# Attention and MLP on one core: exponentials of 54 score tiles written back into PSUM, with engines, buffers and order chosen anew

## The chip, the cores and the metric

The kernel runs on one core of a Trainium2 chip. The metric is the device time of one execution in microseconds (us), as the median of several runs; lower is better. The engines are named as in the profile: PE (TensorE, with PEld for its weight loads), DVE (VectorE), ACT (ScalarE), POOL (GpSimd) and SP (SyncE, which here issues every DMA).

## The reference

Four sequences of 576 tokens, eight heads of width 64, then an MLP of 512 to 2048 to 512:

```python
q_rot, k_rot = rotate(q), rotate(k)                   # rotary embedding
scores = (1 / np.sqrt(64)) * q_rot @ k_rot.T
scores = scores - scores.max(-1)
attn = np.exp(scores); attn = attn / (attn.sum(-1) + 1e-9)
x = (attn @ v)                                        # as [2304 tokens, 512]
h = x @ w_in
out = (s * np.maximum(h, 0) ** 2 + b) @ w_out         # [2304, 512]
```

## The kernel before

**Tiles.** Two heads of one sequence make a pair `pr` (16 pairs). A pair has nine score tiles `i`: eight of 128 query rows by 576 keys, and a ninth (`i` = 8) that holds the last 64 rows of both heads. That is 144 tiles. Tokens are grouped into nine MLP units of 256 tokens; a unit can start when the attention of its tokens is done.

**One score tile.** `s_tile` (L1298) multiplies on PE into one of two score buffers `s` in PSUM, each of two banks. `s_max` (L1324, DVE) scales the scores in place and gives the negative maximum `nm`. `s_exp` (L1330, ACT) takes the exponentials into a buffer `p` in SBUF and sums them into `sum`; when it ends, the score buffer is free for the next tile. `p_s` and `p_r` (L1336, L1344) make `r`, the reciprocal of the sum, in the place of `sum`. For 124 of the tiles, p times r is then split into two fp16 halves: `p_a` (L1356, on ACT, DVE or POOL by a table) writes the high half, `p_b` (L1361, always DVE) writes the remainder, both into `pab`. A DMA transpose, `p_t` (L1368), turns `pab` into `pt`, and `pv_sum` (L1384, PE) multiplies with v. The other 20 tiles, called G in the code (L773: the 16 tiles of unit 0 and the tiles 4 to 7 of pair 0), go another way in fp32: `p_norm`, `p_T` on PE, `p_ev`, `pv32`. All instructions on ACT that the helper `act` records carry its line, L1062; DVE's go by the helpers' L1054, L1056 and L1059.

**Preparation.** Every two pairs share staging buffers `st_q`, `st_k`, `st_v`. q and k are rotated (`rotate`, four instructions), scaled and split (`qk_hi`, `qk_lo`), transposed by DMA and copied with halves swapped (`swap_k`, into `kS`). The weights arrive as 64-bit values in a buffer `w64` and are turned into fp32 by `w_sign` (POOL), `w_rebias` and `w_f32` (DVE), later halved into fp16 pairs (`w_hi`, `w_lo`).

**MLP.** For each of 16 column blocks `f`, `mlp_in` (12 matmuls, L1514; unit 0 in fp32, L1511), then for each two blocks Relu and Square on ACT (`mlp_r`), `g_hi` and `g_lo` (the fp16 halves) and `mlp_out` (L1551).

**Order.** When the kernel is built, `plan` (L684) makes a list of work items, each with an engine, a cost, a due time and the tokens and buffers it reads and writes. `schedule` (L890) then goes through time with these costs and always gives a free engine the ready item with the earliest due time. The order it finds is written out as each engine's fixed instruction stream. The table `PRM` holds offsets of due times and, in `PRM['eng']`, the engine of single items; `BUFS` holds the numbers of buffers: one each for staged `k` and `q`, four for `p`, three for `g`, nine for `vS`.

Of the kernel before, what the change touches and what calls it, by code (L numbers as in the profile page):

```python
# [7 lines left out]
F32 = mybir.dt.float32  # L8
# [19 lines left out]
PRM = {'z0': -0.31,  # L28
 'z1': 0.75,
 'd': 2.86,  # L30
 'ld': -6.32,
 's_lead': 50.37,
 'pab': -0.63,
 'pvlag': -9.44,
 'W0': 5.5,
 'W1': 26.24,
 'Wd': 0.37,
 'wld': 49.09,
 'sq': -6.66,
 'WP': -4.92,  # L40
 'WPd': -2.52,
 'm0': -53.68,
 'x_lead': 54.8,
 'r_lead': 78.68,
 'outlag': 5.0,
 'bias': -24.48,
 'look': 0.034124466599701066,
 'tab': -80.57,
 'fq': (0,),
 'nF': 25,  # L50
 'vz': -4.4,
 'du': [0.25, -5.14, -4.7, -3.11, -3.9, 42.96, -2.92, 5.19, 22.68],
 'ud': 20.54,
# [12 lines left out]
         ('g_lo', 3, 12): 'DVE',  # L66
# [4 lines left out]
         ('g_lo', 8, 12): 'POOL',  # L71
         ('g_lo', 2, 0): 'POOL',
         ('g_hi', 0, 4): 'DVE',
# [5 lines left out]
         ('g_hi', 7, 0): 'DVE',  # L79
         ('g_hi', 4, 14): 'ACT',  # L80
         ('g_hi', 3, 14): 'DVE',
         ('g_hi', 5, 14): 'DVE',
# [19 lines left out]
         ('g_lo', 8, 0): 'DVE',  # L102
         ('g_lo', 7, 2): 'DVE',
# [32 lines left out]
         ('g_hi', 4, 8): 'DVE',  # L136
         ('g_hi', 1, 4): 'ACT',
         ('g_hi', 8, 10): 'ACT',
         ('x_hi', 7): 'ACT',
# [8 lines left out]
         ('g_hi', 6, 2): 'DVE',  # L148
# [3 lines left out]
         ('g_hi', 5, 12): 'ACT',  # L152
         ('g_lo', 5, 12): 'DVE',
         ('x_hi', 6): 'DVE',
         ('g_hi', 6, 8): 'DVE',
         ('g_hi', 8, 2): 'ACT',
         ('g_hi', 7, 12): 'DVE',
         ('g_hi', 8, 14): 'DVE',
         ('g_hi', 0, 8): 'ACT',
         ('g_hi', 8, 8): 'ACT',  # L160
         ('g_hi', 8, 4): 'DVE',
# [17 lines left out]
         ('g_lo', 7, 10): 'POOL',  # L179
# [3 lines left out]
         ('g_hi', 0, 2): 'ACT',  # L183
# [17 lines left out]
         ('w_rebias', 0, 4): 'POOL',  # L201
         ('g_lo', 4, 10): 'POOL',
         ('g_lo', 6, 6): 'DVE',
         ('g_lo', 8, 14): 'DVE',
         ('g_lo', 5, 14): 'DVE',
         ('g_hi', 0, 12): 'DVE',
         ('g_hi', 0, 0): 'ACT',
         ('w_rebias', 1, 1): 'ACT',
         ('w_rebias', 0, 0): 'ACT',
# [4 lines left out]
         ('g_lo', 3, 2): 'POOL',  # L214
# [5 lines left out]
         ('g_lo', 5, 4): 'POOL',  # L220
# [3 lines left out]
         ('g_hi', 2, 14): 'ACT',  # L224
         ('x_hi', 4): 'DVE',
# [19 lines left out]
         ('g_lo', 2, 4): 'POOL',  # L245
         ('w_rebias', 0, 3): 'POOL',
         ('w_rebias', 0, 13): 'ACT',
# [7 lines left out]
         ('g_lo', 7, 6): 'POOL',  # L255
# [4 lines left out]
         ('g_hi', 6, 14): 'ACT',  # L260
# [5 lines left out]
         ('w_rebias', 1, 15): 'POOL',  # L266
# [3 lines left out]
         ('p_ev', 0, 2): 'DVE',  # L270
# [11 lines left out]
         ('p_norm', 0, 2): 'ACT',  # L282
# [6 lines left out]
         ('w_rebias', 1, 10): 'ACT',  # L289
# [5 lines left out]
         ('rotate', 13, 'k'): 'DVE',  # L295
         ('rotate', 13, 'q'): 'DVE',
         ('g_hi', 5, 10): 'DVE',
# [6 lines left out]
         ('p_s', 3, 2): 'DVE',  # L304
         ('p_s', 8, 7): 'ACT',
         ('p_a', 8, 2): 'POOL',
         ('p_a', 15, 5): 'POOL',
         ('p_a', 4, 1): 'ACT',
         ('p_a', 13, 6): 'ACT',
         ('v_hi', 2): 'ACT',  # L310
         ('v_hi', 15): 'DVE',
         ('p_a', 13, 2): 'DVE',
         ('p_a', 11, 2): 'ACT',
         ('p_a', 8, 8): 'DVE',
         ('p_a', 13, 4): 'POOL',
# [5 lines left out]
         ('p_s', 10, 4): 'DVE',  # L321
# [4 lines left out]
         ('p_s', 14, 8): 'DVE',  # L326
         ('p_s', 9, 5): 'ACT',
         ('p_s', 11, 1): 'DVE',
         ('p_s', 6, 1): 'ACT',
         ('p_a', 11, 1): 'POOL',  # L330
# [55 lines left out]
         ('qk_hi', 13, 'q'): 'ACT',  # L386
# [4 lines left out]
         ('p_a', 14, 0): 'ACT',  # L391
         ('p_s', 0, 1): 'DVE',
         ('v_hi', 0): 'ACT',
         ('p_a', 7, 7): 'POOL',
         ('w_hi', 0, 7): 'ACT',
         ('p_s', 15, 3): 'ACT',
         ('p_a', 14, 3): 'DVE',
# [4 lines left out]
         ('p_s', 13, 1): 'ACT',  # L402
# [4 lines left out]
         ('p_a', 10, 1): 'ACT',  # L407
         ('p_s', 15, 6): 'DVE',
         ('p_a', 5, 8): 'DVE',
         ('p_a', 13, 5): 'POOL',  # L410
         ('p_a', 14, 6): 'POOL',
         ('p_s', 10, 7): 'ACT',
# [52 lines left out]
         ('p_s', 10, 6): 'DVE',
         ('p_s', 12, 4): 'DVE',
# [1169 lines left out]
```

## Time and profile before

| | |
|---|---|
| Median of 3 runs (lowest, highest) | 693.55 us (692.4, 694.84) |
| The profiled execution: time | 690.18 us |
| The profiled execution: span from first to last instruction | 688.4 us |
| Busy in the span: PE, DVE, ACT, POOL | 618.3, 508.0, 397.5, 166.3 us |
| Granted TensorE clock, mean | 0.954 |

The profiled execution took 1.8 us more than its span, and 3.4 us less than the median of the runs. Busy times count the time in which an engine had at least one instruction in work; matmuls overlap, so their mean duration is longer than their share of busy time. The clock is the share of full speed that was granted to TensorE. A releaser (the name behind an arrow) is what ended an idle time.

### The profile page before, as it was taken

Reading aid. Unit: us, or ns where it says so; the run is one execution under the profiler, and the core shown is the slowest. Engines: PE = TensorE matmul, PEld = TensorE weight load, DVE = VectorE, ACT = ScalarE, POOL = GpSimd, SP = SyncE. Lnnn points to the kernel's source line nnn. Section 1 sums busy time; section 2 is a strip of 40 time slices with the busy share of each in tenths; the row PEclk is TensorE's granted clock in tenths of the full one; section 3 lists DMA queues with packets and bytes.
Section 4 is the critical chain, followed back from the end, with each engine's and each line's share of the span. In section 5 each row is a group of like instructions: output and inputs, shape, how many; then the busy total and the mean of one; then the engine's idle time right before and its main releaser. Section 6 shows DMA issues by size and latency. Waiting matters only on the chain.

```text
span 688.4 us, 13122 instructions
## 1 busy us (share of the span) xinstructions
PE 618.3 (90%) x4854; PEld 399.5 (58%) x4854; DVE 508.0 (74%) x1214; ACT 397.5 (58%) x842; POOL 166.3 (24%) x162
## 2 busy tenths in 40 slices
PE   1866669999997989799999899989999999999997
PEld 1543335655565655476666466656756666676664
DVE  4389878897999997999998699889959992110301
ACT  2535447766656878578676676856646552343221
POOL 1632373311420336020114111141121030111010
PEclk9996559999999999999999899999999999999999
DMA  7475762689765589579789656988585663000100
GB/s 205 111 187 175 193 169 81 146 148 228 198 136 130 111 187 177 118 147 201 151 192 204 110 102 138 187 165 134 119 146 87 118 131 60 1 31 1 31 0 31
DMA packets 223887, 89.33 MB, mean 130 GB/s; under 512 B 193616, under 2 KB 218320, under 8 KB 223824
## 3 DMA queue, kind: packets, MB, share of 16 engines
q1 hardware_dynamic: 223824, 88.51, 60.1%
q8 instruction: 38, 0.62, 0.4%
q14 instruction: 25, 0.20, 0.1%
HBM read 31.82 MB, written 4.72 MB: 53 GB/s over the span
## 4 chain that ended last, share of the span: by engine, by line
PE 41%; DVE 9%; DMA 7%; SPq 3%; ACT 3%; issue 2%; POOL 0%; DVEq 0%; ACTq 0%
PE po L1551 17%; PE px L1514 15%; DMA pt<-pab 5%; PE px L1392 5%; PE s L1320 3%; DVE s L1327 2%; DVE pab L1059 2%; DMA st_v<-in_v_dram 1%; SPq L1192 1%; ACT hr L1062 1%; SPq L1204 1%; ACT p L1062 1%; DMA vS<-v 1%; ACT junk L1062 1%; SPq L1267 1%
## 5 line engine op out<-in xcount | busy, mean ns | idle before, releaser
L1551 PE MATMUL po<-wio,g 128*128 128x512 f16 x768 | 188.2, 381 | 0.0
L1514 PE MATMUL px<-xa,wio 128*128 128x256 f16 x1536 | 186.3, 273 | 0.0
L1514 PEld LDWEIGHTS <-wio 128*128 128x128 f16 x1536 | 148.4, 98 | 37.2 <-issue 1.7
L1062 ACT ACTIVATE p<-s,nm 128x576 f32<-128x576 f32 x144 | 105.7, 734 | 68.9 <-DVE s L1327 38.6
L1327 DVE TENSOR_SCALAR_CACHE_REDUCE s<-s,es 128x576 f32<-128x576 f32 x135 | 108.9, 814 | 6.8 <-PE s L1321 6.5
L1551 PEld LDWEIGHTS <-g 128*128 128x128 f16 x768 | 71.0, 99 | 70.4 <-issue 3.6
L1059 DVE SCALAR_TENSOR_TENSOR pab<-p,sum,pab 128x576 f16<-128x576 f32 x124 | 104.5, 851 | 9.9 <-POOL pab L1056 6.6
L1535 POOL TENSOR_TENSOR g<-hr,g 128x512 f16<-128x512 f32 x36 | 46.5, 1292 | 210.8 <-ACT g L1062 93.6
L1062 ACT ACTIVATE hr<-px,xc 128x512 f32<-128x512 f32 x64 | 43.8, 684 | 90.0 <-PE px L1514 90.0
L1392 PE MATMUL px<-pt,v 128*64 128x256 f16 (+1 forms) x860 | 53.8, 251 | 14.7 <-DMA pt<-pab 12.8
L1320 PE MATMUL s<-qkT 128*128 128x512 f16 (+1 forms) x150 | 55.2, 407 | 10.3 <-ACT p L1062 10.1
L1320 PE MATMUL s<-kS,qkT 128*128 128x512 f16 (+1 forms) x150 | 55.3, 405 | 9.4 <-DMA kS<-qkT 9.4
L1062 ACT ACTIVATE pab<-p,sum 128x576 f16<-128x576 f32 x64 | 49.0, 768 | 22.5 <-DVE sum L1346 9.4
L1059 DVE SCALAR_TENSOR_TENSOR wio<-w,wio 128x512 uint32<-128x512 uint32 x64 | 49.3, 782 | 10.5 <-POOL wio L1056 10.4
L1392 PEld LDWEIGHTS <-v 128*64 128x64 f16 x860 | 37.7, 112 | 32.2 <-issue 19.6
L1320 PEld LDWEIGHTS <-qkT 128*128 128x128 f16 (+1 forms) x300 | 29.3, 105 | 45.4 <-issue 15.2
L1056 POOL TENSOR_SCALAR pab<-p,sum 128x576 f16<-128x576 f32 x26 | 21.8, 840 | 133.8 <-DVE sum L1346 59.9
L1056 POOL TENSOR_SCALAR wio<-w 128x512 f32<-128x512 f32 x32 | 26.0, 813 | 88.3 <-DMA w<-in_moe_w_in_dram 45.4
L1062 ACT ACTIVATE hr<-hr 128x512 f32<-128x512 f32 x72 | 45.1, 626 | 1.2
L1416 DVE CAST g<-hr 128x512 f16<-128x512 f32 x29 | 13.0, 448 | 43.9 <-ACT hr L1062 43.8
L1535 DVE TENSOR_TENSOR g<-hr,g 128x512 f16<-128x512 f32 x28 | 20.7, 741 | 29.1 <-ACT g L1062 29.0
L1321 PEld LDWEIGHTS <-qkT 128*128 128x128 f16 (+1 forms) x300 | 28.3, 104 | 16.3 <-issue 12.7
(139 smaller groups left out, 926.0 us busy)
## 6 DMA issues: line engine op xcount, KB each, us to landing
w<-in_moe_w_in_dram SPq DMA_DIRECT2D x16, 512.0 KB, 4.5
w<-in_moe_w_out_dram SPq DMA_DIRECT2D x16, 512.0 KB, 4.1
kS<-qkT SPq DMA_DIRECT2D x30, 144.0 KB, 2.7
st_k<-in_k_dram SPq DMA_DIRECT2D x16, 256.0 KB, 3.1
st_q<-in_q_dram SPq DMA_DIRECT2D x16, 256.0 KB, 3.3
st_v<-in_v_dram SPq DMA_DIRECT2D x16, 256.0 KB, 4.7
out_dram<-o SPq DMA_DIRECT2D x7, 512.0 KB, 2.6
vS<-v SPq DMA_DIRECT2D x32, 64.0 KB, 2.3
```

Source lines behind the costliest of these rows:

```text
L1056: eng.tensor_scalar(out=out, in0=in0, scalar1=s1, scalar2=s2, op0=op0, op1=op1)
L1059: nc.vector.scalar_tensor_tensor(out=out, in0=in0, scalar=scalar, in1=in1, op0=op0, op1=op1)
L1062: nc.scalar.activation(out=out, in_=in_, func=func, **kw)
L1192: nc.sync.dma_start(out=t[:, 0, 0:8].rearrange("p (h t) d -> p h (t d)", h=2), in_=main.rearrange("h (p t) d -> p h (t d)", t=4))
L1320: nc.tensor.matmul(ps[rows, MAIN:2 * MAIN], lhs, kk[:, 4 * h:4 * h + 4], start=(n == 0), stop=(n == 1))
L1321: nc.tensor.matmul(ps[rows, MAIN - TAIL:MAIN], lhs, kk[:, 8, 64 * h:64 * h + 64], start=(n == 0), stop=(n == 1))
L1327: nc.vector.tensor_scalar(out=T["s"], in0=T["s"], scalar1=-1.0 / 8.0 if "qF" in st[pr] else st[pr]["es"], scalar2=None, op0=ALU.mult, op1= ...
L1392: nc.tensor.matmul(o[64 * h:64 * h + 64, 0:n], v_rows(pr, h, k, z), pv_rhs(pr, i, h, k), start=((z, k) == todo[0]), stop=((z, k) == todo[-1]))
L1416: nc.vector.tensor_copy(out, in_)
L1514: nc.tensor.matmul(ph, w16[0][:, f, wz, cc], X["xa"][:, xz, c], start=(c == 0 and n == 0), stop=(c == NC - 1 and n == 2))
L1535: (nc.vector if eng == DVE else nc.gpsimd).tensor_tensor(out=g[:, 1], in0=r, in1=g[:, 0], op=ALU.subtract)
L1551: nc.tensor.matmul(po, g[:, gz, jj], w16[1][:, f, wz], start=(f == 0 and i == 0), stop=(f == NF - 1 and i == 2))
```

## The change

1. `s_exp` takes a place `at`. Where the table says `PS`, the exponentials go back over the scores: `T["p"] = T["s"]`, in PSUM. Both `p_a` and `p_b` then read PSUM, and they list the score buffer among what they use, so that it is free only after `p_b`. For `PS`, `p_a` runs on ACT or DVE (POOL entries become ACT).
2. The table has 65 `PS` entries. Eleven of them are tiles of G, for which the code sets `SB`; so 54 of the 124 split tiles are in PSUM, 70 keep `p` in SBUF.
3. `BUFS`: `k` and `q` 1 to 2, `p` 4 to 3, `g` 3 to 2, `vS` 9 to 4; the others stay.
4. Due-time offsets in `PRM` are new, the latencies and two rates that `schedule` uses too, and many engine entries. `nF` goes from 25 to 22, which leaves the same 20 tiles in G. The number of matmuls and of DMAs does not change.

Counted over all items, the engines change so (before to after):

| step | ACT | DVE | POOL |
|---|---|---|---|
| `p_a`, p in SBUF | 64 to 50 | 34 to 7 | 26 to 13 |
| `p_a`, p in PSUM | 0 to 47 | 0 to 7 | none |
| `p_s` | 62 to 70 | 82 to 74 | none |
| `rotate` | none | 23 to 20 | 9 to 12 |
| `g_hi` | 35 to 33 | 29 to 31 | none |
| `g_lo` | none | 28 to 30 | 36 to 34 |
| `p_ev` | 11 to 13 | 9 to 7 | none |
| `p_norm` | 10 to 9 | 5 to 5 | 5 to 6 |
| `qk_hi` | 21 to 22 | 5 to 5 | 4 to 3 |
| `v_hi` | 13 to 12 | 2 to 2 | 1 to 2 |
| `w_rebias` | 19 to 18 | none | 13 to 14 |

```diff
-PRM = {'z0': -0.31, 'ld': -6.32, 's_lead': 50.37, 'pab': -0.63, 'pvlag': -9.44, 'wld': 49.09, 'm0': -53.68,
- 'x_lead': 54.8, 'r_lead': 78.68, 'bias': -24.48, 'look': 0.034124466599701066, 'nF': 25,
- 'du': [0.25, -5.14, -4.7, -3.11, -3.9, 42.96, -2.92, 5.19, 22.68], 'ud': 20.54, 'sbt': 5.22,
+PRM = {'z0': -2.03, 'ld': -2.77, 's_lead': 51.82, 'pab': -0.7, 'pvlag': -14.21, 'wld': 19.1, 'm0': 0.57,
+ 'x_lead': 68.78, 'r_lead': 117.69, 'bias': -60.48, 'look': 0.02, 'nF': 22,
+ 'du': [0.25, -5.0, -4.72, -0.78, -4.34, 55.9, 3.61, 33.52, 20.04], 'ud': 20.46, 'sbt': 2.1,
...
-         ('p_a', 8, 3): 'DVE',
+         ('p_at', 13, 5): 'PS',
+         ('p_at', 5, 0): 'SB',
...
-BUFS = {'k': 1, 'q': 1, 'v': 2, 'z': 2, 'p': 4, 'pab': 4, 'pt': 2, 'x': 2, 'xa': 2, 'r': 3, 'g': 3, 'w64': 2, 'v16': 4, 'qkT': 4, 'kS': 4, 'vS': 9}
+BUFS = {'k': 2, 'q': 2, 'v': 2, 'z': 2, 'p': 3, 'pab': 4, 'pt': 2, 'x': 2, 'xa': 2, 'r': 3, 'g': 2, 'w64': 2, 'v16': 4, 'qkT': 4, 'kS': 4, 'vS': 4}
...
-DVE_RATE, POOL_RATE = .42, .66
+DVE_RATE, POOL_RATE = .37, .62
...
-        add(n + .2, ACT, .72, "s_exp", *c, r=[("s", c), ("nm", c)], w=[("p", c)])
+        G = i < 8 and slot_of[pr, i | 3] < PRM["nF"]
+        at = "SB" if G else pick("p_at", c, "SB")
+        pk, ps = ("p" if at == "SB" else "pp", c), [] if at == "SB" else [("s", c)]
+        add(n + .2, ACT, .72 if at == "SB" else .70, "s_exp", *c, at, r=[("s", c), ("nm", c)], w=[pk])
...
-            add(z, e, None, "p_a", *c, e, r=[("p", c), ("r", c)], p=[("pab", c)])
-            add(z + .1, DVE, .73, "p_b", *c, r=[("p", c), ("r", c)], w=[("pab", c)])
+            e = ACT if ps and e == POOL else e
+            add(z, e, (.67 if e == ACT else .73) if ps else None, "p_a", *c, e, r=[pk, ("r", c)] + ps, p=[("pab", c)])
+            add(z + .1, DVE, .73 if at == "SB" else .75, "p_b", *c, r=[pk, ("r", c)] + ps, w=[("pab", c)])
+            work[-1] = {**work[-1], "port": int(at == "SB")}
...
-    def s_exp(pr, i):
+    def s_exp(pr, i, at):
         T = tiles[pr, i]
-        T["sum"] = small("sum%d" % slots["p"], 1, 1)
-        T["p"] = new(pp, "p", [P, 576], F32)
+        T["sum"] = small("sum%d" % slots["p"] if at == "SB" else "psum%d" % T["slot"], 1, 1)
+        T["p"] = new(pp, "p", [P, 576], F32) if at == "SB" else T["s"]
         act(T["p"], T["s"], AF.Exp, bias=T["nm"], scale=-1.0, accum_out=T["sum"])
```

## Rows read from the trace of the kernel before

**Rows 1.** The page: the line of the span, the busy time of each engine, and the slices of PE, DVE, ACT and the clock (40 equal slices, 17.2 us each; a digit is the busy share in tenths).

```profile
span 688.4 us, 13122 instructions
PE 618.3 (90%) x4854; PEld 399.5 (58%) x4854; DVE 508.0 (74%) x1214; ACT 397.5 (58%) x842; POOL 166.3 (24%) x162
PE   1866669999997989799999899989999999999997
DVE  4389878897999997999998699889959992110301
PEclk9996559999999999999999899999999999999999
```

**Rows 2.** Busy time by stage: the stretch, its length, busy time of PE, PEld, DVE, ACT and POOL with the number of instructions, the granted clock, the busy share of the DMA engines and GB/s.

```profile
0.00:50.00 50.00, 28.97 (x136) 18.08 (x136) 26.92 (x63) 19.91 (x40) 20.32 (x24) 1.00 0.64 169
50.00:100.00 50.00, 30.95 (x157) 16.54 (x157) 41.91 (x89) 23.36 (x51) 20.93 (x23) 0.59 0.65 179
100.00:565.00 465.00, 439.60 (x3732) 285.84 (x3733) 417.54 (x1025) 315.89 (x694) 111.92 (x105) 0.98 0.73 149
565.00:689.00 124.00, 118.83 (x834) 78.99 (x830) 21.65 (x40) 38.36 (x60) 13.14 (x11) 0.99 0.09 23
```

**Rows 3.** PE's waits between 100 and 565 us: who waited for whom, us in total, times, longest.

```profile
PE px L1392 <- DMA pt<-pab: 12.8, 12, 2.1
PE s L1320 <- ACT p L1062: 8.0, 8, 3.6
PE px L1392 <- ACT bcs L1062: 1.7, 1, 1.7
PE px L1072 <- ACT junk L1062: 0.9, 1, 0.9
```

**Rows 4.** Groups of instructions of the whole span, each shape apart: line, engine, operation, out<-in, shapes, number | busy us, mean ns of one | idle before, and what ended it. These are the steps of the score tiles.

```profile
L1327 DVE TENSOR_SCALAR_CACHE_REDUCE s<-s,es 128x576 f32<-128x576 f32 x135 | 108.9, 814 | 6.8 <-PE s L1321 6.5
L1059 DVE SCALAR_TENSOR_TENSOR pab<-p,sum,pab 128x576 f16<-128x576 f32 x124 | 104.5, 851 | 9.9 <-POOL pab L1056 6.6 <-ACT pab L1062 2.8
L1062 ACT ACTIVATE pab<-p,sum 128x576 f16<-128x576 f32 x64 | 49.0, 768 | 22.5 <-DVE sum L1346 9.4 <-issue 6.1 <-DMA pt<-pab 3.0
L1054 DVE TENSOR_SCALAR pab<-p,sum 128x576 f16<-128x576 f32 x34 | 20.5, 604 | 1.6 <-DMA pt<-pab 1.5
L1062 ACT ACTIVATE sum<-sum 128x1 f32<-128x1 f32 x62 | 12.0, 197 | 0.6
L1056 DVE TENSOR_SCALAR sum<-sum 128x1 f32<-128x1 f32 x82 | 11.5, 145 | 3.8 <-ACT p L1062 3.5
```

**Rows 5.** The same view: instructions that read PSUM as the changed steps will, and two of ACT, from PSUM and from SBUF.

```profile
L1059 DVE SCALAR_TENSOR_TENSOR o<-po,xc,bcs 128x512 f32<-128x512 f32 x16 | 11.4, 746 | 13.7 <-PE po L1551 13.6
L1416 DVE COPY pt<-po 128x640 f32<-128x640 f32 x9 | 7.4, 823 | 4.4 <-PE po L1428 3.6 <-PE px L1392 0.8
L1062 ACT ACTIVATE hr<-px 128x512 f32<-128x512 f32 x8 | 4.7, 588 | 2.1 <-PE px L1511 2.1
L1062 ACT ACTIVATE hr<-hr 128x512 f32<-128x512 f32 x72 | 45.1, 626 | 1.2
```

**Rows 6.** The same view: steps that change their engine.

```profile
L1416 DVE CAST g<-hr 128x512 f16<-128x512 f32 x29 | 13.0, 448 | 43.9 <-ACT hr L1062 43.8
L1535 DVE TENSOR_TENSOR g<-hr,g 128x512 f16<-128x512 f32 x28 | 20.7, 741 | 29.1 <-ACT g L1062 29.0
L1243 DVE TENSOR_TENSOR z<-st_k,tab 128x576 f32<-128x576 f32 x13 | 11.4, 878 | 5.2 <-POOL st_k L1249 2.9 <-DMA st_q<-in_q_dram 2.3
L1245 DVE TENSOR_TENSOR st_k<-st_k,tab 128x576 f32<-128x576 f32 x13 | 9.7, 750 | 0.0
L1247 DVE TENSOR_TENSOR st_k<-st_k,z 128x288 f32<-128x288 f32 x13 | 6.3, 484 | 0.0
L1249 DVE TENSOR_TENSOR st_k<-st_k,z 128x288 f32<-128x288 f32 x13 | 5.9, 451 | 0.0
```

**Rows 7.** One score tile in the timeline, near 303 us (start us, duration us, engine, line, operation): its first matmul on PE, its exponential and high half on ACT, its low half on DVE.

```profile
303.22 0.38 PE L1320 MATMUL s<-qkT 128*128 128x512 f16 x1
...
306.84 0.20 ACT L1062 ACTIVATION_READ_ACCUMULATOR p<-s,nm 128x1 f32 x1
308.78 0.76 ACT L1062 ACTIVATE pab<-p,sum 128x576 f16<-128x576 f32 x1
310.68 0.82 DVE L1059 SCALAR_TENSOR_TENSOR pab<-p,sum,pab 128x576 f16<-128x576 f32 x1
```

**Rows 8.** The exponentials between 100 and 565 us, as a group of the stage.

```profile
L1062 ACT ACTIVATE p<-s,nm 128x576 f32<-128x576 f32 x132 | 96.9, 735 | 63.3 <-DVE s L1327 35.7 <-DVE sum L1346 17.1 <-DVE xi L1486 3.8
```

**Rows 9.** The start: loads of staged k in SP's timeline (the first for pair 1, the second for pair 2), and the score matmuls of PE that waited for `kS` at 77 and 94 us.

```profile
11.72 0.43 SPq L1192 DMA_DIRECT2D st_k<-in_k_dram  x1
36.38 0.37 SPq L1192 DMA_DIRECT2D st_k<-in_k_dram  x1
80.45 0.61 PE L1320 MATMUL s<-kS,qkT 128*128 128x512 f16 x1 [3.15 <-DMA kS<-qkT]
95.14 0.61 PE L1320 MATMUL s<-kS,qkT 128*128 128x512 f16 x1 [1.30 <-DMA kS<-qkT]
```

**Rows 10.** The chain that ended last, near 624 us, in order of time (start, us, engine, what): one `mlp_in` block and the matmuls of `mlp_out` between two.

```profile
623.94 1.31 PE px L1514 x12
625.25 1.29 PE po L1551 x6
```

More of the change, by code (lines that the diff above doesn't have):

```diff
@@ L65 @@
          ('g_lo', 7, 4): 'DVE',
-         ('g_lo', 3, 12): 'DVE',
+         ('g_lo', 3, 12): 'POOL',
          ('g_lo', 4, 2): 'POOL',
@@ L70 @@
          ('g_lo', 6, 14): 'DVE',
-         ('g_lo', 8, 12): 'POOL',
+         ('g_lo', 8, 12): 'DVE',
          ('g_lo', 2, 0): 'POOL',
-         ('g_hi', 0, 4): 'DVE',
+         ('g_hi', 0, 4): 'ACT',
          ('rotate', 2, 'q'): 'DVE',
@@ L147 @@
          ('p_norm', 2, 1): 'DVE',
-         ('g_hi', 6, 2): 'DVE',
+         ('g_hi', 6, 2): 'ACT',
          ('x_hi', 8): 'DVE',
@@ L182 @@
          ('rotate', 8, 'k'): 'DVE',
-         ('g_hi', 0, 2): 'ACT',
+         ('g_hi', 0, 2): 'DVE',
          ('g_hi', 6, 0): 'DVE',
@@ L254 @@
          ('p_norm', 0, 1): 'ACT',
-         ('g_lo', 7, 6): 'POOL',
+         ('g_lo', 7, 6): 'DVE',
          ('g_lo', 8, 6): 'DVE',
@@ L269 @@
          ('p_norm', 3, 0): 'ACT',
-         ('p_ev', 0, 2): 'DVE',
+         ('p_ev', 0, 2): 'ACT',
          ('p_ev', 1, 0): 'ACT',
@@ L294 @@
          ('p_norm', 3, 2): 'ACT',
-         ('rotate', 13, 'k'): 'DVE',
+         ('rotate', 13, 'k'): 'POOL',
          ('rotate', 13, 'q'): 'DVE',
-         ('g_hi', 5, 10): 'DVE',
+         ('g_hi', 5, 10): 'ACT',
          ('p_ev', 0, 7): 'ACT',
@@ L320 @@
          ('v_hi', 1): 'ACT',
-         ('p_s', 10, 4): 'DVE',
+         ('p_s', 10, 4): 'ACT',
          ('p_s', 12, 8): 'ACT',
@@ L401 @@
          ('p_s', 7, 6): 'ACT',
-         ('p_s', 13, 1): 'ACT',
+         ('p_s', 13, 1): 'DVE',
          ('p_s', 6, 7): 'DVE',
@@ L406 @@
          ('p_s', 2, 1): 'ACT',
[L407 to L412, printed above, removed]
+         ('p_s', 15, 6): 'ACT',
+         ('p_s', 10, 7): 'DVE',
          ('w_hi', 0, 2): 'ACT',
@@ L561 @@
          ('p_s', 10, 3): 'ACT',
-         ('p_s', 14, 2): 'ACT',
+         ('p_s', 14, 2): 'DVE',
          ('p_s', 14, 6): 'DVE',
-         ('p_a', 7, 2): 'POOL',
          ('p_s', 9, 3): 'DVE',
@@ new lines @@
+         ('p_a', 5, 6): 'ACT',
+         ('p_a', 11, 5): 'ACT',
+         ('p_a', 4, 6): 'POOL',
+         ('p_at', 13, 3): 'SB',
+         ('p_a', 1, 7): 'POOL',
+         ('p_a', 9, 6): 'ACT',
+         ('p_a', 10, 7): 'POOL',
+         ('p_a', 11, 0): 'ACT',
+         ('p_a', 13, 8): 'ACT',
+         ('p_at', 10, 7): 'SB',
+         ('p_at', 3, 7): 'SB',
+         ('p_s', 0, 6): 'DVE',
+         ('p_at', 2, 7): 'SB',
+         ('p_a', 2, 4): 'ACT',
+         ('p_a', 13, 4): 'ACT',
+         ('p_a', 6, 1): 'ACT',
```

597 lines of the change are left out of this document (357 added, 240 removed).

## The prediction, made before the changed kernel had run

> **What bounds the kernel now.** I read the page first: PE is busy for 618.3 of 688.4 us, and in the slices its idle time lies at the start, where DVE is not full either and the clock falls to five tenths [rows 1]. Then the stages. From 565 us on there is no attention left: PE works 118.8 of 124 us, and the chain there is `mlp_in` and `mlp_out` in turn, 1.31 us and 1.29 us, nothing between them [rows 2, 10]. One MLP unit costs 16 x 2.60 = 41.6 us there, so three units are left when attention ends. In the long middle, 100 to 565 us, two engines are near full: PE idles for 25.4 us of 465 and DVE for 47.5 us (10.2%); ACT idles for 149 us and POOL for 353 us [rows 2]. The first 100 us hold 59.9 us of busy PE, half of it at a clock of 0.59, the mixture of 1.2 and 2.4 GHz [rows 2].
>
> The number of matmuls stays, so PE's work is a constant and the time can only change by PE's idle time: 40 us in the first 100 us, 25 us in the middle, 5 us at the end. In the middle the waits name two causes: 12.8 us for transposed halves of p, which come behind `p_b` on DVE, and 8.0 us for a score buffer that an exponential still holds [rows 3]. These two, and the start, are what the change can reach.
>
> **DVE gets lighter.** The profiled durations [rows 4 to 6] give: `p_a` now 34 x 0.604 = 20.5 us; after it 7 x 0.604 in SBUF and 7 in PSUM. No `p_a` from PSUM is in the trace; the copy of 640 elements out of PSUM takes 0.823, which scaled to 576 is 0.741. So 4.2 + 5.2 = 9.4, a gain of 11.1. `rotate`: 3 x (0.878 + 0.750 + 0.484 + 0.451) = 7.7 gained. `p_s` 8 x 0.145 = 1.2 and `p_ev` 2 x 0.823 = 1.6 gained; `g_hi` 2 x 0.448 and `g_lo` 2 x 0.741 cost 2.4. Together 19.2 us.
>
> `p_b` from PSUM is not in the trace either. The nearest rows: the same operation out of PSUM with 512 elements, 0.746, or 0.839 if scaled by length; and `s_max`, 576 elements read from PSUM, 0.814. I take 0.814, the row with the same length, against 0.851 now: 54 x 0.037 = 2.0 us gained, ends 0.6 and 5.7. DVE loses some 21 us, and nearly all of it in the middle, where I count 20.
>
> The rows say that a read from PSUM costs `p_b` nothing, while it costs `p_a` on DVE 0.14 us each. A page speaks against the change: the Trainium skill, "VectorE: DVE Perf Modes", section "Rules for kernel authors", advises to copy out of PSUM first where many operations follow. If that held for `p_b` too, at the same 0.14 us, DVE would lose 12 us and not 21, and the term below would be -2.4 and not -3.8.
>
> What the 20 us are worth: DVE's idle time in the middle grows from 47.5 to 67.5 us, 1.42 times. I assume that waits behind a queue shrink as its idle share grows (an estimate; no row shows it): 12.8 / 1.42 = 9.0, **-3.8 us**. Its ends are 0, if PE's static order gives the wait back elsewhere, and -20, a rival below.
>
> **ACT gets heavier.** 33 more `p_a` x 0.768 = 25.3, 8 `p_s` x 0.197 = 1.6; the other moves cancel within 1 us. A read from PSUM seems cheaper for ACT, 0.588 against 0.626, so 47 x 0.038 = 1.8 comes back. An exponential written to PSUM has no row; I take no change, with 54 x 0.038 = 2 us either way. ACT's idle time falls from 149 to 124 us. What waits for ACT alone on PE, 1.7 + 0.9 [rows 3], grows by 1.2: **+0.5 us**. If ACT were full, this would be a new bound; at 340 of 465 us it isn't.
>
> **Score buffers are held longer.** This is the wait that the change adds. Now a score buffer is free after the exponential; the tile in the timeline holds it from 303.22 to 307.04, 3.8 us. With p in PSUM it is held until `p_b` ends, for this tile at 311.50: 4.5 us more, of which 1.6 are `p_a` and `p_b` themselves and 2.9 is waiting in the queues of ACT and DVE [rows 7]. The ends are 1.6 and 4.5. I take 3.0, the work and half of the waiting, since DVE's queue gets shorter and a late `p_b` can be ordered forward. There are 132 exponentials in the middle [rows 8]: 132 x 3.82 = 504 us on two buffers, 54% of the stage. With 54 x 3.0 = 162 more it is 72%; the buffers' idle share falls from 46% to 28%, and the wait grows by 1.61. With the DVE factor: 8.0 / 1.42 x 1.61 = 9.1, **+1.1 us**. At 1.6 it would be -0.9, at 4.5 it would be +5.1. Behind the waiting score matmul in PE's stream stand MLP blocks that cannot pass it; behind it also waits `s_max` on DVE, and later `p_t` on SP.
>
> **The start.** With a second buffer for staged k and q, pair 2's load need no longer wait until pair 0's k is split: SP issued pair 1's at 11.72 us and pair 2's only at 36.38 [rows 9]. PE waited 3.15 and 1.30 us for `kS` at 77 and 94 us [rows 9], pairs 2 and 3 by their place. Ends: nothing, if rotation and splitting are late anyway, and all 4.4. I take all of it, as DVE is only half busy in the first 50 us [rows 2]: **-4.4 us**. The weight loads' due times move behind some of these loads on SP's queue; unless the conversion then runs out of weights, this is covered by the same idle time of DVE, and I count it as the end at zero.
>
> **Nothing for the rest.** `p` with three buffers serves 90 tiles and not 144: at about 5.4 us each (from 0.73 us before 306.84 to 311.50 [rows 7, 8]) that is 162 us per buffer, before it was 194. `vS` beyond four could not be used, as the four `v16` buffers have the same last reader. `g` with two: a block of two `f` takes PE 5.2 us [rows 10] and `g_hi` and `g_lo` 1.2 [rows 6], so the next g is ready in time; without that cover it would cost 1.2 us a block. Three more rotations go to POOL, which has 353 us idle; their price is a later `qk_hi`, behind the same cover. Later due times for units 5 to 8 move MLP work of fixed length.
>
> **Sum.** -3.8 + 0.5 + 1.1 - 4.4 = -6.6. The profiled execution took 690.18 us, so 683.6 there. That execution was 3.4 us below the median, 693.55; as a median I forecast **687 us**, with 684 to 691 as its own range.
>
> **Rivals.**
> *The score buffers bind.* PE waits for `s`, and DVE's relief is used up. The sum is zero when the wait reaches 15.7 us: 5.6 x 2.8, an idle share of 16%, an extra hold of 5.1 us a tile. At 5.7 us the buffers are 87% used, the wait is 20 us, and the time 690.2 + 4.5, as a median **698 us**; up to 702 at 6.0 us. For it: the one tile shown is at 4.5 already, and only two buffers serve. Against: 54% used now, and PE's waits for `s` are just 8.0 us [rows 3]. The Trainium skill, "PSUM — Partial Sum Buffer", section "Summary: rules for kernel authors", asks to evacuate promptly; by that rule this is the case to expect.
> *DVE was the bound.* If the middle ends earlier by all that DVE loses, PE having the same work and fewer holes: -20 with the start's gain inside it, **674 us**. For it: in the slices DVE is as full as PE for most of the middle [rows 1]. Against: PE has only 25.4 us of idle time there, so nearly every hole would have to close.
> *Nothing reaches the end.* PE is 94.5% busy in the middle and the order is static: a hole closed opens again at the next block. **693.5 us**. To it belongs the case that the change isn't what its table says: only 54 of 65 entries act, and if ACT's queue eats the gain little is left.
>
> **Chances.** Forecast 0.47, DVE as the bound 0.14, nothing 0.11, score buffers (with any other new wait of that size) 0.28. A difference under 0.3% (2.1 us) can't be told from none here. So faster 0.61, same 0.11, slower 0.28. The range reaches from below the second rival, 669, to the first rival's upper end, 702; less than two in ten lie outside.
>
> **What would show it.** DVE's busy time near 487 us and ACT's near 422; `p_b` on `s` at 0.81 and `p_a` on DVE from PSUM at 0.74; PE's waits for `pt` near 9 us in the middle; its waits for `s` near 9 us, now ended by `p_b`; no wait for `kS` near 80 us. I am wrong if PE's waits for `s` pass 16 us, if `p_b` out of PSUM takes over 0.85, or if attention ends after 565 us.

## The result and the profile after

The changed kernel takes **698.22 us** (median of 6 runs, 697.06 to 703.19) beside 692.97 for the kernel before (6 runs): a ratio of **1.0092, 95% interval [1.0062, 1.0121]**. It is slower by 0.9%; 687 us was forecast. The profiled execution took 697.06 us, its span 695.3. A second measurement of the same two kernels, under run 7, gave a smaller loss, 0.4%.

The page after: span, busy times, and the slices of PE, DVE and the clock (17.4 us each).

```profile
span 695.3 us, 13156 instructions
PE 614.4 (88%) x4854; PEld 397.6 (57%) x4854; DVE 508.4 (73%) x1176; ACT 419.2 (60%) x881; POOL 167.4 (24%) x161
PE   0953749989897899999999799999999999999997
DVE  3587998898899988987888788887978884211111
PEclk9995558999999899999999999999999999999999
```

DVE's busy time did not fall: 508.4 beside 508.0 [rows 1]. The dent at the start is deeper. Busy time by stage, columns as in [rows 2]:

```profile
0.00:50.00 50.00, 26.79 (x132) 16.70 (x133) 29.65 (x69) 20.90 (x42) 20.62 (x25) 1.00 0.66 176
50.00:100.00 50.00, 26.44 (x138) 15.27 (x139) 44.78 (x79) 20.25 (x43) 28.35 (x26) 0.54 0.68 175
100.00:565.00 465.00, 435.51 (x3696) 281.87 (x3694) 402.84 (x966) 333.30 (x723) 105.48 (x99) 0.98 0.74 146
565.00:696.00 131.00, 125.66 (x894) 83.81 (x890) 31.08 (x64) 44.78 (x76) 12.93 (x11) 0.99 0.14 31
```

PE is busy for 53.2 us in the first 100, 6.7 less than before, and for 4.1 us less in the middle. DVE and POOL have more to do in the first 100 us, by 5.6 and 7.7 us; DVE's 14.7 us less in the middle stand against that and 9.4 us more behind 565, where attention now lasts until 580 (the last `p_b` ends at 580.3 us, before at 567.0).

PE's waits between 100 and 565 us:

```profile
PE px L1526 <- DMA pt<-pab: 10.8, 10, 3.6
PE s L1454 <- ACT p L1196: 5.0, 6, 2.0
PE s L1454 <- DMA kS<-qkT: 3.0, 1, 3.0
...
PE s L1454 <- DVE pab L1193: 0.7, 1, 0.7
```

The list is cut: waits of PE for other things, of 2.0 us and less, are left out. For `kS` there was one wait of 2.5 us before in the same stretch, which [rows 3] does not show. PE waited for a score buffer that `p_b` held once, for 0.7 us. So neither the forecast's +1.1 nor the rival's 20 us is there. The groups of the changed steps:

```profile
L1193 DVE SCALAR_TENSOR_TENSOR pab<-p,sum,pab 128x576 f16<-128x576 f32 x70 | 60.8, 871 | 4.3 <-ACT pab L1196 3.1 <-POOL pab L1190 0.9
L1193 DVE SCALAR_TENSOR_TENSOR pab<-s,psum,pab 128x576 f16<-128x576 f32 x54 | 43.6, 810 | 8.5 <-ACT pab L1196 8.3
L1196 ACT ACTIVATE p<-s,nm 128x576 f32<-128x576 f32 x90 | 66.2, 736 | 38.5 <-DVE s L1461 21.4 <-DVE sum L1480 5.9 <-PE po L1562 3.3
L1196 ACT ACTIVATE s<-s,nm 128x576 f32<-128x576 f32 x54 | 38.3, 709 | 24.3 <-DVE s L1461 11.2 <-DVE sum L1480 5.2 <-DVE xi L1620 3.1
L1196 ACT ACTIVATE pab<-s,psum 128x576 f16<-128x576 f32 x47 | 34.4, 733 | 6.1 <-DMA pt<-pab 2.7 <-DVE psum L1480 1.8 <-ACT x L1196 0.9
L1188 DVE TENSOR_SCALAR pab<-s,psum 128x576 f16<-128x576 f32 x7 | 5.7, 813 | 0.3 <-DMA pt<-pab 0.3
```

The prices were nearly as forecast: `p_b` from PSUM 0.810 (forecast 0.814), `p_a` on ACT from PSUM 0.733 (0.730); only `p_a` on DVE was dearer, 0.813 (0.741), and there are seven of them.

**Where the time goes.** I counted PE's work from the matmul records: the columns that a matmul moves, divided by 2.4 GHz, counted twice for fp32, and in proportion where a matmul uses fewer than 128 output columns. This is a measure for comparing kernels, not a duration; it comes to about 537 us for each of them. The table shows when each kernel had begun equal work (us from the span's start), and the starts of two exponentials, counted from 0; number 8 is the first of pair 2. "Mended" is a run below:

| work done | before | after | before, buffers of after | after, one k/q buffer | mended start (two runs) |
|---|---|---|---|---|---|
| 10 | 45.2 | 44.0 | 46.2 | 43.7 | 47.4, 45.1 |
| 25 | 98.2 | 108.4 | 110.8 | 99.0 | 103.0, 101.0 |
| 60 | 146.7 | 155.3 | 163.3 | 145.4 | 154.6, 152.8 |
| 150 | 252.3 | 266.0 | 271.8 | 252.2 | 266.3, 266.5 |
| 200 | 315.0 | 322.6 | 329.7 | 326.6 | 321.4, 322.4 |
| 300 | 430.9 | 440.3 | 440.7 | 440.1 | 437.9, 438.5 |
| 530 | 676.6 | 683.4 | 686.2 | 688.3 | 680.3, 681.2 |
| exponential 8 | 83.1 | 95.5 | 97.6 | 85.5 | 84.0, 82.3 |
| exponential 24 | 134.5 | 148.0 | 153.7 | 135.4 | 149.4, 147.6 |

At 25 us of work the changed kernel is 10.2 us late, and at 530 it is 6.8 us late. On balance nothing more is lost between these in this profile, and 3.4 us come back; what brings them is not shown. Single profiles of one kernel differ here by some 3 us (run 7 has a second one of the changed kernel).

How the start became late, in lines of the changed kernel's timelines from 12 to 64 us: SP loads k of pair 2 and later transposes pair 1's; DVE rotates pair 2's k and q (L1377 to L1383) and splits pair 1's (`nat`, `qk_lo`); PE waits for a bank that ACT has yet to copy out (`x`), then for pair 1's `kS`.

```profile
12.87 0.47 SPq L1326 DMA_DIRECT2D st_k<-in_k_dram  x1
50.17 3.33 SPq L1401 DMA_TRANSPOSE qkT<-nat  x1
57.82 1.15 SPq L1410 DMA_DIRECT2D kS<-qkT  x2
...
39.61 0.75 DVE L1377 TENSOR_TENSOR z<-st_k,tab 128x576 f32<-128x576 f32 x1
44.27 0.82 DVE L1383 TENSOR_TENSOR st_k<-st_k,z 128x288 f32<-128x288 f32 x1
46.43 0.80 DVE L1193 SCALAR_TENSOR_TENSOR nat<-st_k,sc,nat 128x576 f16<-128x576 f32 x1
48.34 0.80 DVE L1193 SCALAR_TENSOR_TENSOR nat<-st_q,sc,nat 128x576 f16<-128x576 f32 x1
...
52.26 1.01 PE L1254 MATMUL px<-wio 128*128 128x128 bf16 x8 [6.24 <-ACT x L1196]
63.68 0.61 PE L1454 MATMUL s<-kS,qkT 128*128 128x512 f16 x1 [6.44 <-DMA kS<-qkT]
```

The same splits, the `kS` copies and PE's wait for them in the kernel before:

```profile
35.51 0.80 DVE L1059 SCALAR_TENSOR_TENSOR nat<-st_k,sc,nat 128x576 f16<-128x576 f32 x1
42.93 0.81 DVE L1059 SCALAR_TENSOR_TENSOR nat<-st_q,sc,nat 128x576 f16<-128x576 f32 x1
51.17 1.16 SPq L1276 DMA_DIRECT2D kS<-qkT  x2
55.30 0.61 PE L1320 MATMUL s<-kS,qkT 128*128 128x512 f16 x1 [2.40 <-DMA kS<-qkT]
```

The second buffer does what it says: pair 2's load goes out at 12.87, not at 36.38 [rows 9]. But the rotation of pair 2 has an earlier due time than the last splits of pair 1. Before, its data were missing and the splits of k and q (35.51 and 42.93 us) went first or beside its first step. Now the data are there, DVE takes the rotation first, and pair 1's splits come at 46.43 and 48.34, its `kS` copies at 57.82 in place of 51.17. PE waits 6.44 us for them where it waited 2.40, and later pairs follow: the wait at 90 us is 2.63 where it was 3.15 at 77. All waits for `kS` up to 110 us come to 12.1 us, before to 6.9. The wait of 6.24 us before them is not in the kernel before, but the `kS` of pair 1 landed only near 63 us, so without it PE would have waited there for longer. The missing buffer had been an ordering of the work.

### The profile page after: what moved, and what is told of

Its sections match the earlier page's. It is cut to its first block, busy times and chain, and to the rows that moved or that the text cites. A ratio compares the mean times of both kernels' runs of the same rounds, so it can differ in the third digit from the quotient of the medians.

```text
span 695.3 us, 13156 instructions
## 1 busy us (share of the span) xinstructions
PE 614.4 (88%) x4854; PEld 397.6 (57%) x4854; DVE 508.4 (73%) x1176; ACT 419.2 (60%) x881; POOL 167.4 (24%) x161
## 4 chain that ended last, share of the span: by engine, by line
PE 49%; DMA 6%; DVE 3%; issue 1%; ACT 1%; SPq 1%; DVEq 0%; ACTq 0%
PE po L1685 19%; PE px L1648 18%; PE px L1526 6%; PE s L1454 5%; DMA pt<-pab 4%; DVE s L1461 1%; DMA qkT<-nat 1%; DVE pab L1193 1%; PE s L1455 1%; DMA st_v<-in_v_dram 1%; ACT hr L1196 0%; SPq L1338 0%; DVE g L1669 0%; PE px L1206 0%; DVE nat L1193 0%
## 5 line engine op out<-in xcount | busy, mean ns | idle before, releaser
L1669 POOL TENSOR_TENSOR g<-hr,g 128x512 f16<-128x512 f32 x34 | 42.9, 1263 | 261.5 <-ACT g L1196 163.3
L1196 ACT ACTIVATE p<-s,nm 128x576 f32<-128x576 f32 x90 | 66.2, 736 | 38.5 <-DVE s L1461 21.4
L1454 PE MATMUL s<-kS,qkT 128*128 128x512 f16 (+1 forms) x150 | 54.4, 399 | 12.1 <-DMA kS<-qkT 12.1
L1193 DVE SCALAR_TENSOR_TENSOR pab<-p,sum,pab 128x576 f16<-128x576 f32 x70 | 60.8, 871 | 4.3 <-ACT pab L1196 3.1
L1193 DVE SCALAR_TENSOR_TENSOR wio<-w,wio 128x512 uint32<-128x512 uint32 x64 | 52.2, 819 | 12.2 <-POOL wio L1190 12.2
L1454 PEld LDWEIGHTS <-qkT 128*128 128x128 f16 (+1 forms) x300 | 28.6, 104 | 48.4 <-issue 14.0
L1196 ACT ACTIVATE s<-s,nm 128x576 f32<-128x576 f32 x54 | 38.3, 709 | 24.3 <-DVE s L1461 11.2
L1193 DVE SCALAR_TENSOR_TENSOR pab<-s,psum,pab 128x576 f16<-128x576 f32 x54 | 43.6, 810 | 8.5 <-ACT pab L1196 8.3
L1196 ACT ACTIVATE hr<-hr 128x512 f32<-128x512 f32 x72 | 45.2, 628 | 1.2
L1196 ACT ACTIVATE pab<-p,sum 128x576 f16<-128x576 f32 x50 | 38.1, 768 | 8.6 <-DVE sum L1480 4.6
L1196 ACT ACTIVATE pab<-s,psum 128x576 f16<-128x576 f32 x47 | 34.4, 733 | 6.1 <-DMA pt<-pab 2.7
```

The source lines that it names most:

```text
L1193: nc.vector.scalar_tensor_tensor(out=out, in0=in0, scalar=scalar, in1=in1, op0=op0, op1=op1)
L1196: nc.scalar.activation(out=out, in_=in_, func=func, **kw)
L1454: nc.tensor.matmul(ps[rows, MAIN:2 * MAIN], lhs, kk[:, 4 * h:4 * h + 4], start=(n == 0), stop=(n == 1))
L1669: (nc.vector if eng == DVE else nc.gpsimd).tensor_tensor(out=g[:, 1], in0=r, in1=g[:, 0], op=ALU.subtract)
```

## The experiments

A ratio is to the kernel before on the same chip, with its 95% interval.

**1. Only the buffers.** The kernel before with the changed kernel's numbers of buffers, the order made anew; all p in SBUF.

```diff
-BUFS = {'k': 1, 'q': 1, ... 'p': 4, ... 'g': 3, ... 'vS': 9}
+BUFS = {'k': 2, 'q': 2, ... 'p': 3, ... 'g': 2, ... 'vS': 4}
```

> The kernel before, everything in SBUF, with the buffer counts of the changed kernel alone (k and q 2, p 3, g 2, vS 4); order found anew. If the second buffer crowds the start: the fifth exponential at 63 to 67 us and the ninth at 93 to 97 though nothing is in PSUM, and the time 697 or more. If holding the score buffers costs the time: start as before, at or under 693.

1.005 [1.0016, 1.0083]. Its first score matmul that needs pair 1's `kS`:

```profile
65.44 0.61 PE L1320 MATMUL s<-kS,qkT 128*128 128x512 f16 x1 [7.14 <-DMA kS<-qkT]
```

The late start is there with no exponential in PSUM and all due times of before: 12.6 us late at 25 us of work, with 13.1 us of waits for `kS` up to 110. The buffers make it, without the rest of the change; which of the four, this run doesn't say.

**2. One buffer for k and q.** The changed kernel, order made anew.

```diff
-BUFS = {'k': 2, 'q': 2,
+BUFS = {'k': 1, 'q': 1,
```

> The changed kernel with one buffer for staged k and q, as before the change; the order is found anew. If the second buffer crowds the start: the fifth exponential at 57 to 60 us (65 in the changed kernel), the ninth at 83 to 87 (95), and the time 690 to 693, unless the new order of the rest is worse by itself, which the distance between the tenth and the last exponential tells. If holding the score buffers costs the time: the start may move, the time stays at 697 or above.

1.0134 [1.0073, 1.0196]. The start is as before (99.0 us at 25, and 252.2 at 150 us of work). Pair 1's k is split ahead of pair 2's rotation again:

```profile
37.96 0.80 DVE L1193 SCALAR_TENSOR_TENSOR nat<-st_k,sc,nat 128x576 f16<-128x576 f32 x1
...
44.70 0.75 DVE L1377 TENSOR_TENSOR z<-st_k,tab 128x576 f32<-128x576 f32 x1
```

Then 11.7 us are lost between 150 and 200. In that order, PE waits between 100 and 565 us for score buffers held by `p_b`:

```profile
PE s L1454 <- DVE pab L1193: 6.7, 4, 2.9
```

So the start follows from the k and q buffers; but with the start as before this kernel is no faster than the changed one: an order made anew for that reason brought a new loss.

**3. That order kept, p beside it in SBUF.** The kernel of run 2, whose free room holds two more fp32 buffers, one for each score buffer.

```diff
-T["p"] = new(pp, "p", [P, 576], F32) if at == "SB" else T["s"]
+T["p"] = new(pp, "p", [P, 576], F32) if at == "SB" else pp.tile([P, 576], F32, tag="pe%d" % T["slot"], ...)
```

> The changed kernel with one buffer each for staged k and q, as in the run with that edit alone (ratio 1.0134, about 702 us, with 6.7 us of PE waiting for score buffers that p_b still held, and 11.6 us lost between 250 and 327 us). The order stays exactly as in that run, but the 54 exponentials go into two buffers in SBUF of their own, so a score buffer is free after its exponential. If holding score buffers is what it loses there: 690 to 696 us, and no waits of PE for s ended by DVE. If the loss lies in the order: 700 to 703 us, and the 11.6 us stay.

1.0068 [1.004, 1.0097], between the two expectations. The waits on `pab` are gone, but the time between 150 and 200 us of work stays (255.2 to 329.6). In the profiles nothing is won (spans of 700.2 and 701.6 us); the ratios lie 0.7% apart with intervals that overlap. Whether holding cost a part of run 2 stays open; the 11.7 us are the order's.

**4. The changed kernel's order kept, p in SBUF.** The same edit in the changed kernel; with two k and q buffers there is room for fp16 only.

> The changed kernel with every engine's order kept, but the 54 exponentials go to two SBUF buffers of their own (rounded to fp16 there, since fp32 doesn't fit), so a score buffer is free after the exponential again. If holding the score buffers costs the time: DVE's waits for scores fall from 24 us to under 10 and the time falls by 5 to 7 us, to about 692. If the loss is made in the first 100 us by the order of the preparation: the time stays at 697 to 699, the exponentials of the start stay where they were (the fifth at 65 us, the ninth at 95).

1.0089 [1.005, 1.0128], the changed kernel's own ratio. PE no longer waits for `pab` on `s`; its other waits stay (11.4 us for `pt`, 6.1 for `s` behind an exponential). Holding the score buffers cost nothing in this order. But the order was made for a kernel that holds them; whether the plan would come out shorter without the hold, no run shows, here or in run 8.

**5. The activation table early.** ACT's table load stands behind a load of `st_v` until 14.1 us in the changed kernel, since its first work, a `w_rebias`, went to POOL. A small Square is put ahead.

```diff
     nc.vector.memset(ones16, 1.0)
+    act(small("warm", 1, 1), ones32[:, 0:1], AF.Square)
```

> The changed kernel in the same order, with one tiny activation at the very start, so that ACT loads its table before the first v has landed. If the start sets the time: the first matmul comes at about 14.5 us and not 16.3, and 1.3 to 1.9 us of it reach the end, about 696.5. If holding the score buffers sets it: the 1.9 us are lost again behind the next wait, 698 as before.

1.0086 [1.0055, 1.0117]. PE reaches 2 us of work at 19.9 and not 21.9, and 5 us of work at 31.0 and not 29.9. The lead is gone at once, and the table is not the cause.

**6. DVE's relief alone.** The kernel before, its order kept, with DVE's 34 `p_a` on ACT.

```diff
-cast(eng, T["pab"][:, 0:576], T["p"], T["r"])
+cast(ACT if eng == DVE else eng, T["pab"][:, 0:576], T["p"], T["r"])
```

> The kernel before, its order kept, with the 34 high halves p_a of DVE on ACT: DVE loses 34 x 0.604 = 20.5 us and ACT gets 34 x 0.768 = 26.1 us, as the change does for its greater part, without PSUM, new buffers or a new order. By the prediction's terms (relief of DVE -3.8, ACT +0.5): 690 us, PE's waits for pt near 9 us in the middle. If DVE bound the middle: 675 to 680 us. If the relief is worth nothing in a fixed order, or ACT's queue takes it: 693 to 697 us.

0.9997 [0.9975, 1.002]. The page, the group of `p_a` on ACT and PE's wait for `pt` in the middle:

```profile
PE 617.9 (89%) x4854; PEld 398.4 (58%) x4854; DVE 491.1 (71%) x1180; ACT 418.2 (61%) x876; POOL 161.9 (23%) x162
...
L1062 ACT ACTIVATE pab<-p,sum 128x576 f16<-128x576 f32 x98 | 74.5, 767 | 24.9 <-DVE sum L1346 9.9 <-issue 7.3 <-DMA pt<-pab 4.4
...
PE px L1392 <- DMA pt<-pab: 10.4, 9, 2.5
```

DVE is busy for 16.9 us less, ACT for 20.7 more, and the time stays. The wait for `pt` fell by 2.4 us, and PE's busy time in the middle is 440.05 where it was 439.60 [rows 2]: a hole closed there opened elsewhere. In this order that speaks against the forecast's term, and against the rival in which DVE was the bound. The run pays for the relief with work on ACT, as the forecast's sum did (-3.8 and +0.5); a lighter DVE without a heavier ACT, or in an order planned for it, was not tried.

**7. A mended start.** The changed kernel, planned twice: in the second pass each item is due when it began in the first, but the attention of pairs 1, 2 and 3, with what it needs, is due 5, 17 and 11 us earlier and the loads for pairs 4 and 5 five us later (the lines for these loads are left out below).

```diff
+    first = {1: 5.44, 2: 17.06, 3: 10.99}
+    for i, x in enumerate(work):
+        x["t"] = begun[i]
+        if x["fn"] in ATTEND and x["a"][0] in first and x["a"][1] < 4:
+            x["t"] -= first[x["a"][0]]
...
+                work[i]["t"] = min(work[i]["t"], work[m]["t"] - took(work[i]))
```

> The changed kernel, its order made a second time with each item's own start in the first order as its due time, but the attention of the pairs 1, 2 and 3 (and what it needs) due 5, 17 and 11 us earlier and the loads for pairs 4 and 5 five us later. What is moved lies in the first 100 us; buffers, engines and PSUM as in the change. If the late start is what the change lost: exponential 8 near 81 us in place of 95, and 690 to 693 us in all. If the start only shows a loss that other work would bring anyway: the exponentials 4 to 12 earlier by 5 to 12 us, the 24th and later ones as in the changed kernel, and 697 to 700 us.

0.9984 [0.9962, 1.0007]: no loss against the kernel before. On the same chip, run 5, which is the changed kernel but for one small instruction, stood at 1.0086. Two of its matmuls that wait for `kS`, of pairs 1 and 2:

```profile
60.33 0.58 PE L1459 MATMUL s<-kS,qkT 128*128 128x512 f16 x1 [2.64 <-DMA kS<-qkT]
80.73 0.61 PE L1459 MATMUL s<-kS,qkT 128*128 128x512 f16 x1 [2.44 <-DMA kS<-qkT]
```

PE waits 2.64 us and not 6.44 for pair 1, and pair 2 comes 12 us earlier. But exponential 24 stands at 149.4 us, no earlier than in the changed kernel (148.0): that was the mark of the second expectation, while the time is near that of the first. Since this kernel and the changed one had not been measured side by side, both ran again on one chip:

> The changed kernel itself, once more, so that it stands on the same chip beside the three kernels that follow. 1.007 to 1.011 of the kernel before.

> The mended start once more, now beside the changed kernel. If the start is what the change lost, all of the 0.9% goes: 0.995 to 1.001 of the kernel before, 5 to 8 us under the changed kernel. If it is only part of it, as the single profiles suggest (692.2 against 695.3 us of span): 1.003 to 1.006.

The changed kernel 1.0036 [1.0007, 1.0065], the mended start 1.0007 [0.9976, 1.0039]. The first came out under its expectation of 1.007 to 1.011. The medians differ by 1.6 us here, and the intervals overlap; the profiles differ by 5.2 us of span (698.2 and 693.0), by the first pair of profiles it was 3.1. So the change's loss is 0.4 to 0.9%, and with the mended start none is left that can be measured against the kernel before.

That the late start is what the change loses at its end is not shown by this. The changed kernel's second profile reads 109.2, 266.8, 443.6 and 686.4 us at 25, 150, 300 and 530 us of work. With it, the mended start's lead is 5 to 8 us at 25 us of work, nothing at 150, and 2 to 5 us behind 300. What leads behind 300 has arisen after the early lead was gone, and the mended start is itself a new order of the whole kernel (run 9 shows what that can do). What holds the changed order at 266 us, early start or late, stays open.

**8. The mended start with p in SBUF,** its order kept, with the edit of run 4; twice, the second time beside run 7's second.

> The kernel of the run with the mended start, its order kept, but the 54 exponentials go into two fp16 buffers in SBUF of their own, as in the first such run: no score buffer is held for p, and p_a and p_b read SBUF. If PSUM brings something once the start is mended (cheaper reads for ACT, no port shared with POOL): 696 to 699 us. If it brings and costs nothing: 694 to 695 us, as with PSUM. If holding costs: 690 to 692 us.

> The mended start with its exponentials in SBUF once more, in the order of the run beside it. If the place in PSUM brings something: 0.3 to 0.6% slower than with PSUM. If it brings nothing and costs nothing: within 0.2% of it.

1.0034 [1.0002, 1.0067], then 1.0 [0.9974, 1.0026]. On the one chip where both ran, SBUF is 1.4 us ahead, and the intervals overlap widely: in this order the place of the exponentials brings nothing and costs nothing that shows.

**9. A new order and nothing else.** The kernel before with one due-time offset nudged, `W1` by 0.3 in one run and `z1` by 0.2 in another.

```diff
- 'W1': 26.24,
+ 'W1': 26.54,
```

> The kernel before, with one due-time offset moved by 0.3 (W1, that of the second weight matrix, 26.24 to 26.54), and the order of all engines made anew from it. The same buffers, engines and operations, nothing in PSUM, the same start up to the 24th exponential. If the time follows from the work of the engines, it is that of the kernel before, 693 us within 2. If it follows from how the order happens to fall (the theory that the change lost its gain in the new order, not in its parts), 697 to 705 us, with the loss where the order departs, behind 125 us.

> The kernel before with another single due-time offset moved by a little (z1, that of the preparation of the later sequences, 0.75 to 0.95) and its order made anew; nothing else. If any new order costs about what the change lost, as the first such run has it (1.0114): 1.004 to 1.015. If that run was an unlucky one: 0.998 to 1.002.

1.0114 [1.0076, 1.0152] and 1.0142 [1.0101, 1.0184]. Both starts are near that of before (100.1 and 98.0 us at 25 us of work). Busy time from 200 to 300 us, the first nudge and the second, each in its own profile:

```profile
200.00:300.00 100.00, 84.78 (x614) 51.94 (x612) 89.77 (x216) 67.00 (x142) 26.82 (x23) 0.95 0.65 132
```

```profile
200.00:300.00 100.00, 85.55 (x629) 53.33 (x629) 92.97 (x219) 68.13 (x141) 29.12 (x23) 0.93 0.68 143
```

The kernel before has PE busy for 89.85 us there. In the first run PE's waits for `s` behind an exponential rise from 8.0 [rows 3] to 17.2 us in the middle. An order made anew cost as much as the whole change, with no engine given more work. Both nudges came out slower than the kernel before; that a nudge can also come out faster, no run here shows.

**10. A better order for the changed kernel?** Run 7 with 123 shifts of due times over the whole kernel.

```diff
+MOVES = [
+    (('tile', 2, 6), 2.2),
...
+]
...
+    for (kind, p0, p1), dt in MOVES:
```

> The kernel of the run with the mended start (ratio 0.9984), with 123 shifts of due times over the whole kernel on top, chosen so that the planner's own order ends earlier; the same buffers, engines, operations and PSUM tiles. If the order is what holds the changed kernel back in the middle too: 684 to 691 us, faster than both kernels, with PE's idle time between 100 and 565 us under 22 us (26.2 in the run it starts from). If the planner's costs don't carry over to the chip at this size: 692 to 698 us.

0.9976 [0.9938, 1.0014]: not told apart from the kernel before, nor from run 7. At 25 us of work it is at 99.6 us, the start all but mended (98.2 before); at 150 it is at 266.9 again, and PE's waits for `pt` rose to 15.6 us. PE idles for 30.2 us in the middle, more than the 26.2 it set out from. No version was found that surely beats the kernel before.

## Why the prediction was wrong

**The start, forecast at -4.4 us, is the step that failed.** It measured +10.2 us at 25 us of work, and PE's waits for `kS` up to 110 us went from 6.9 to 12.1 us in place of vanishing. The working saw the effect of the load rightly (it moved from 36.38 to 12.87), but its ends ran from -4.4 to nothing, so that a loss was excluded; its reason was that DVE is half busy in the first 50 us [rows 2]. But the slices from 34 to 69 us, where pair 1's splits stand, read 8 and 9 for DVE [rows 1]. And the question which queue the load was moved past was asked of SP, not of DVE: what has its data earlier is also taken earlier, ahead of what PE waits for. The kernel's due times showed it: rotation of pair 2 stands ahead of `qk_lo` of pair 1. Runs 1 and 2 show the buffers of k and q as the cause of the late start, and the order on DVE as its way. How much of the 5.25 us at the end is due to it stays open: run 2 has the start of before and is no faster for it, and run 7's lead is gone at 150 us of work.

**DVE's relief, forecast at -3.8 us, was nothing.** Its size was right in its first term: `p_a` on DVE takes 9.6 us and not 20.5, as forecast 11 less. `p_b` with 60.8 + 43.6 = 104.4 us is where it was, since the 70 that read SBUF are dearer on average, 871 beside 851 ns [rows 4]. `rotate` gave 1.2 us and not 7.7: three fewer on DVE, but the rest slower, its last step (L1383) 644 and 691 ns for k and q, 451 before for k [rows 6]. Of its last two steps, the 15 that overlap an instruction of POOL take 897 ns in the mean, the other 25 take 444. The conversion of the weights, not counted at all, became dearer in the same way (last section). But the value was wrong too: run 6 takes 16.9 us from DVE in a fixed order and does not move the time, though the wait for `pt` shrinks. The assumption that waits shrink with DVE's idle share had no row, and the text said so; its end at zero is what run 6 shows. The rival in which DVE was the bound (674 us) has the same run against it.

**Held score buffers, forecast at +1.1 us, cost nothing** in this order (0.7 us of waits, and runs 4 and 8). That the result of 698.22 meets the rival's 698 us is luck: that rival had 20 us of waits for `s`, and there are 5.7. Its chance also covered any other new wait of that size, without naming one.

**ACT, +0.5 us:** busy 419.2 us, 422 expected. PE's waits for ACT other than for an exponential went from 2.6 to 4.0 us in the middle. This and the prices, all but that of `p_a` on DVE, were about right.

**The signs.** DVE's busy time (487 expected, 508.4), the wait for `kS` and attention's end (565, now 580) all spoke against the forecast. The named fear, `s` above 16 us, did not come.

**What was not weighed:** that every part of the change is bought with a new order, and that orders of equal work differ by over 1% here (run 9). This belonged in the sum as a term of its own. Whether the new due times by themselves cost something stays open: no run has them with an order made for exponentials in SBUF.

## What to carry to other kernels

A buffer that is too few also orders the work. Before adding one, ask which work it lets in early, and what on that engine PE is waiting for; give that its priority outright. In a kernel whose order is planned by due times, time a nudged plan of the same kernel first: only an effect above that spread can be put down to the part. And in a static order an engine that is 90% busy may still give nothing when it gets lighter, as in run 6: look for the waits that end on it, and where PE stands next.

## What the hardware showed that I had not expected

**`p_b` from PSUM doesn't mind POOL.** Of the 70 `p_b` on SBUF, 14 overlap an instruction of POOL and take 1122 ns in the mean, up to 2029, the other 56 808 ns. Of the 54 on PSUM, 17 overlap one and take 806, the others 812. Two of them beside the rotation on POOL, all lines from the changed kernel's timeline:

```profile
214.18 1.87 POOL L1377 TENSOR_TENSOR z<-st_q,tab 128x576 f32<-128x576 f32 x1
215.99 2.03 DVE L1193 SCALAR_TENSOR_TENSOR pab<-p,sum,pab 128x576 f16<-128x576 f32 x1
216.01 1.39 POOL L1379 TENSOR_TENSOR st_q<-st_q,tab 128x576 f32<-128x576 f32 x1
...
319.00 1.41 POOL L1379 TENSOR_TENSOR st_k<-st_k,tab 128x576 f32<-128x576 f32 x1
319.88 0.82 DVE L1193 SCALAR_TENSOR_TENSOR pab<-s,psum,pab 128x576 f16<-128x576 f32 x1 [1.14 <-ACT pab L1196]
```

The Trainium skill, "SBUF — State Buffer", section "Who interferes with whom", says that a DVE instruction with two SBUF inputs contends with a GpSimd instruction that reads SBUF, and one with at most one SBUF input does not, outside the two-port modes. With p in PSUM only `pab` is left as a large input in SBUF, and the trace agrees. So the gain of a PSUM operand here is not a cheaper read but some 310 ns in the mean of the cases of overlap. Run 4 tests it in the same order: its 54 `p_b` that read fp16 in SBUF cost 919 ns in the mean, against 810; the 18 that overlap POOL take 1131, the other 36 take 814. In run 3, with fp32 in SBUF, 11 take 1067 and 43 take 813.

The same crowding shows in the conversion of the weights, when POOL has more to do (28.35 and not 20.93 us in 50 to 100). Of the 32 `w_f32` instructions in the first 100 us, 20 overlap one of POOL after the change and 14 did before; they take 1079 and 1047 ns in the mean, the others 677 and 683. The group of `w_f32` in the first 100 us, before and after:

```profile
L1059 DVE SCALAR_TENSOR_TENSOR wio<-w,wio 128x512 uint32<-128x512 uint32 x32 | 26.4, 842 | 8.2 <-POOL wio L1056 8.1
```

```profile
L1193 DVE SCALAR_TENSOR_TENSOR wio<-w,wio 128x512 uint32<-128x512 uint32 x32 | 29.6, 928 | 9.9 <-POOL wio L1190 9.9
```

**An exponential into PSUM is cheaper for ACT,** 709 ns beside 736 into SBUF; in run 4 the same 54, written to SBUF, took 735. The forecast had taken no change, with 38 ns either way.
